# Four runs of 18 attention products between the groups of h's products, instead of two runs of 36

## The chip, the cores and the metric

The kernel runs on one core of one Trainium2 chip. The core has a matrix engine (PE, with its weight loads shown apart as PEld), a vector engine (DVE), a scalar engine (ACT), a general engine (POOL) and a synchronising engine (SP) which here issues the DMA transfers. Each engine takes its instructions in the order in which the program was written, and waits at an instruction until the semaphores that it names have been raised by other engines or by landed transfers.

The metric is the device time of one execution, in microseconds (us). Less is better. Beside the times there is one profiled execution, of which the trace keeps every instruction's start and duration.

## The reference

The program computes attention in which small scores are dropped, and feeds its result to a two-layer network. All data are float32.

```python
# attention: 8 batches, 8 heads, 576 tokens, 64 numbers per head
scores = scale * np.matmul(q, k.transpose(0, 1, 3, 2))
thresh = np.max(scores, axis=-1, keepdims=True) - tau
scores = np.where(scores >= thresh, scores, -1000000000.0)
attn   = softmax(scores)                       # over the 576 keys
x      = np.matmul(attn, v)                    # -> 4608 tokens x 512
# network on 4608 tokens: 512 -> 1024 -> 512
h    = x @ w_in
solu = h * softmax(h)
ln   = (solu - mean) / np.sqrt(var + 1e-06) * g_ln
out  = ln @ w_out
```

What this case is about are the products `attn @ v` (called pv here) and `x @ w_in` (called h).

## The kernel before

**Units.** The 576 tokens of a batch are cut into two blocks of 256 and a rest of 64. In the code a unit of attention is (batch `b`, `kind`, pair of heads `hp`): kinds 0 and 1 are the two blocks of 256 tokens, with four pairs of heads each, and kind 2 is the rest of 64 tokens for all eight heads at once. Each unit takes two slots (`slots`, line 367), so a batch has 18 slots and the program 144.

**Rounds.** The main loop (line 820) makes one round per slot. A round first writes PE's score products of its slot (`scores`, line 376), then DVE's row minimum (line 420), ACT's threshold and exponential (lines 435 and 444), POOL's division by the sum for the slot before (lines 451 to 454) and DVE's 32x32 block transposes of that (line 466). When both slots of a unit are transposed, SP issues the transfers that put the blocks in their places in `wT` (lines 475, 477, and 482 for kind 2). The four transfers of line 482 each fill one half of `wT`'s partitions: two fill the lower half, two the upper half. Products with v of the lower half (`u` = 0) wait for the first two, those of the upper half (`u` = 1) for the others.

**What PE does beside the scores.** In each round PE also takes one step of the network: a half of h (`ff_h`, `("h", 0)` and `("h", 1)`) or a half of the output (`ff_o`), in the cycle h, h, o, o. In the rounds with a step of h, when a unit's products with v are due (three rounds after its last slot, line 716), PE takes those as well (`attend_steps`, line 486, 36 instructions for kinds 0 and 1, 72 for kind 2). As a rule h's 16 products come first and all of pv's after them. For kind 2 alone, pv's instructions are handed to `ff_h` as a generator `beside` and drawn from it between h's groups.

**h's groups.** `ff_h` computes 512 of the 1024 columns of h for 128 tokens in four groups (`c` = 0 to 3) of four instructions, each on one 64x64 quarter of the PE array. All instructions around the change work on such quarters, four at a time, and every float32 instruction stands in the trace as two passes, so that 16 instructions of h are 32 records and 36 of pv are 72. The instructions of h are 512 columns long, those of kind 2's pv 64.

**PSUM.** h and pv are accumulated in two buffers of PSUM called p0 and p1 (`take`, line 104), which are handed from user to user in the order in which they are freed. A pv's buffer is freed by ACT's copy of its result (`attended`, line 537), the output's by ACT's copy at line 690, h's by DVE at line 600.

**Fence.** After the first half of h (part 0) POOL writes a small mark (`fence`, line 109) once the last four products are done. The first product of part 1 waits for this mark (line 575). After part 1 DVE takes the row maximum of h (line 585).

The last round's units are taken by an ending (from line 831) in which `ff_h` is called without a split and returns before it draws from `beside`.

Of the kernel before, what the change touches and what calls it, by code (L numbers as in the profile page):

```python
# [20 lines left out]
def kernel(  # L21
# [82 lines left out]
    def take(name):  # L104
        tag = pairs_free.pop(0)
        return tag, ps_mm.tile([P, 1024], F32, tag=tag, name=name)


    def fence(first):
        m = nc.gpsimd.memset(mark, 0.0)  # L110
        for mm in first:
            sync(m, mm)
        return m

    def sync(late, first):
        tc.add_manual_dep(
            late.ins, first.ins.name,
            mybir.DependencyInfo(mybir.DependencyClass.Sync, mybir.DependencyReason.DATA),
            reason="rows change banks",
        )  # L120
# [365 lines left out]
    def attend_steps(key):  # L486
        b, kind, hp = key
        unit = units[key]
        wT = unit["wT"]
        unit["y"] = take("pv")  # L490
        _, y = unit["y"]
        y = y.rearrange("p (u n) -> p u n", u=2)

        for e in range(2) if kind == 2 else [None]:
            for m in range(NK):
                for u in range(2):
                    d, h0 = source(b * NP + (hp if e is None else e + 2 * u))
                    for h in range(2):
                        if e is None:
                            to = y[ROWS[h], u, 0:P].rearrange("p (g r x) -> p g r x", r=2, g=2)  # L500
                            rhs = wT[ROWS[u], :, m, :, h]
                        else:
                            to = y[ROWS[h], u, 64 * e : 64 * e + 64].rearrange(
                                "p (g x) -> p g x", g=2
                            )
                            rhs = wT[ROWS[u], :, m, e, h]
                        nc.tensor.matmul(  # L507
                            out=to,
                            lhsT=d["v"][
                                ROWS[u], (h0 + h - u) % 4, m,  # L510
                            ],
                            rhs=rhs,
                            start=m == 0, stop=m == NK - 1,
                        )
                        yield
# [25 lines left out]
    def tokens(t):  # L541

        if len(t) == 1:
            return xe[t[0]]
        b, kind, m = t
        return xh[b, kind][:, :, P * m : P * m + P]


    def ff_h(t, part, split, beside=()):
        beside = iter(beside)  # L550
        x = tokens(t)
        if part == 0:
            tag, h = take("h_ps")
            ffn[t] = dict(h=h, tag=tag, split=split)
        d = ffn[t]
        h = d["h"]
        if not d["split"]:
            f = slice(512 * part, 512 * part + 512)
            for c in range(NP):
                nc.tensor.matmul(  # L560
                    out=h[:, f], lhsT=x[:, c], rhs=w1_parts[:, c, part],
                    start=c == 0, stop=c == NP - 1,
                )
            return
        last = []
        for c in range(NP):
            for r in range(2):
                f = slice(512 * (part ^ r), 512 * (part ^ r) + 512)
                for y in range(2):
                    mm = nc.tensor.matmul(  # L570
                        out=h[ROWS[y], f], lhsT=x[ROWS[r], c, ROWS[y]], rhs=w1_parts[ROWS[r], c, part ^ r],
                        start=part == 0 and c == 0, stop=part == 1 and c == NP - 1,
                    )
                    if part and not last:
                        sync(mm, d["fence"])
                    last.append(mm)
            for _, _ in zip(range(36 * (c > 1)), beside):
                pass
        if part == 0:
            d["fence"] = fence(last[-4:])  # L580
# [193 lines left out]
    with tc.manual_schedule():  # L774
# [37 lines left out]
        rnd = 0  # L812
# [7 lines left out]
        while True:  # L820
# [84 lines left out]
            beside = ()  # L905
            if attending is not None and attending[1] == 2 and step is not None:
                beside = attend_steps(attending)
            if step == ("h", 0):
                ff_h(cur, 0, rnd + 1 < NS, beside)
                quarter = 1  # L910
            elif step == ("h", 1):
                ff_h(cur, 1, None, beside)
                quarter = 2
                by = rnd + 2 * (rnd == 14)
# [102 lines left out]
```

## Time and profile before

| what | value |
|---|---|
| median of 3 runs | 855.63 us (854.59, 855.63, 858.16) |
| the profiled execution's own time | 855.96 us |
| its span, from the first to the last instruction | 854.2 us |
| PE busy | 819.7 us, 96% of the span |
| DVE, ACT, POOL busy | 680.4, 572.3, 499.1 us (80, 67, 58%) |
| pv's passes of 64 columns | 1152 passes, 21.8 us busy in all |
| h's passes (both forms of line 570) | 2048 passes |
| transfers into `wT`, issue to landing | median 6.7 us (288 KB) and 5.5 us (576 KB) |

The span is what lies between the first and the last instruction on the core; the execution's own time is 1.8 us longer. Busy time of PE counts a stretch in which at least one matmul is in flight; a matmul's record is longer than the step between two matmuls on one quarter, so a short wait need not show as idle time.

Kind 2's pv is found in the trace as the passes of 64 columns on line 507. They stand at eight places, one per batch, which begin at 120.8, 214.0, 308.4, 410.7, 505.7, 609.2, 702.2 and 798.5 us.

### The profile page before, as it was taken

To read this page: it belongs to the slowest core of one execution; us is meant where nothing else is said; L and a number is where in the kernel's file an instruction comes from. 1 tells how busy PE (TensorE), PEld (TensorE's weight loads), DVE (VectorE), ACT (ScalarE), POOL (GpSimd) and SP (SyncE) were. 2 spreads that over 40 slices of the span, in tenths; PEclk is the share of its full clock that TensorE was granted. 3 is DMA by queue.
4 is the path that set the end of the run, shared out by engine and by line. 5 is a ranking of instruction groups with operands and counts; after the bars stand their busy time and mean duration, and the time that the engine had idled before them with its cause. 6 is when DMAs were issued, how large, how long until landed. Compare 5 with 4: busy or idle time off the path is not lost.

```text
span 854.2 us, 36120 instructions
## 1 busy us (share of the span) xinstructions
PE 819.7 (96%) x15363; PEld 613.4 (72%) x15363; DVE 680.4 (80%) x1241; ACT 572.3 (67%) x1127; POOL 499.1 (58%) x945
## 2 busy tenths in 40 slices
PE   6679889999999999999999999999999999999997
PEld 5456666667677787777688877777777777777655
DVE  6999868889788888888788878888888888787361
ACT  6888857877666666666676667766667777775121
POOL 3888637666556656565566666565666655555120
PEclk8889999999999999999999999999999999999999
DMA  9989897898889788887889787888888887655212
GB/s 339 265 236 231 208 206 185 227 250 208 225 208 227 194 191 205 219 214 181 216 212 220 194 177 200 212 212 212 200 207 228 202 195 188 154 136 140 67 39 63
DMA packets 75442, 168.54 MB, mean 197 GB/s; under 512 B 11274, under 2 KB 32786, under 8 KB 75282
## 3 DMA queue, kind: packets, MB, share of 16 engines
q1 hardware_dynamic: 74994, 165.82, 77.3%
q8 instruction: 120, 1.97, 1.0%
q10 hardware_dynamic: 288, 0.43, 0.2%
q14 instruction: 40, 0.33, 0.1%
HBM read 46.14 MB, written 9.44 MB: 65 GB/s over the span
## 4 chain that ended last, share of the span: by engine, by line
PE 80%; DVE 7%; DMA 6%; ACT 3%; issue 2%; POOL 1%; SPq 1%; DVEq 0%; ACTq 0%
PE o_ps L675 27%; PE h_ps L570 21%; PE s_ps L399 15%; PE pv L507 14%; DMA wT<-T 4%; PE h_ps L560 3%; DVE T L466 2%; DVE w L420 2%; ACT w L435 1%; ACT w L444 1%; DVE w L290 1%; DMA V<-u 1%; POOL w L454 0%; PE tp L336 0%; SPq L482 0%
## 5 line engine op out<-in xcount | busy, mean ns | idle before, releaser
L435 ACT ACTIVATE w<-s_ps,nth 128x576 f32<-128x576 f32 x280 | 196.9, 738 | 110.5 <-DVE nth L420 92.0
L675 PE MATMUL o_ps<-w,uT 64*64 64x256 f32 x4608 | 268.4, 376 | 1.3 <-DVE uT L662 0.6
L675 PEld LDWEIGHTS o_ps<-w,uT 64*64 64x64 f32 x4608 | 221.0, 133 | 55.2 <-ACT xh L537 12.0
L420 DVE CUSTOM_DVE_ANT_0 w<-s_ps,tau_t 128x576 f32<-128x576 f32 x280 | 200.1, 751 | 73.7 <-PE s_ps L399 46.3
L454 POOL TENSOR_SCALAR w<-w,sm 128x576 f32<-128x576 f32 x288 | 221.3, 780 | 14.3
L466 DVE STREAM_TRANSPOSE T<-w 128x576 f32<-128x576 f32 x288 | 207.7, 756 | 24.4 <-POOL w L454 23.7
L570 PE MATMUL h_ps<-w,xh 64*64 64x512 f32 x1856 | 220.4, 590 | 0.0
L444 ACT ACTIVATE w<-w,ntau 128x576 f32<-128x576 f32 x288 | 219.5, 766 | 0.0
L507 PEld LDWEIGHTS pv<-wT,v 64*64 64x64 f32 x5760 | 170.4, 135 | 40.7 <-issue 22.9
L399 PE MATMUL s_ps<-kT,qT 64*64 64x64 f32 (+1 forms) x2048 | 173.5, 415 | 16.6 <-ACT w L435 12.5
L507 PE MATMUL pv<-wT,v 64*64 64x128 f32 (+1 forms) x5760 | 173.1, 263 | 7.2 <-DMA wT<-T 5.0
L570 PEld LDWEIGHTS h_ps<-w,xh 64*64 64x64 f32 x1856 | 114.5, 133 | 81.4 <-issue 52.1
L451 POOL TENSOR_SCALAR sm<-sm 128x2 f32<-128x2 f32 x144 | 36.2, 252 | 194.5 <-ACT w L444 191.1
L452 POOL TENSOR_TENSOR sm<-sm,mone 128x2 f32<-128x2 f32 x144 | 108.2, 751 | 12.0
L399 PEld LDWEIGHTS s_ps<-kT,qT 64*64 64x64 f32 x2048 | 70.5, 137 | 25.4 <-ACT w L435 18.0
L537 ACT COPY xh<-pv 128x256 f32<-128x256 f32 x64 | 25.4, 397 | 72.5 <-PE pv L507 72.4
L636 ACT ACTIVATE V<-u,nb,rs 128x1024 f32<-128x1024 f32 x36 | 44.7, 1241 | 41.3 <-POOL nb L626 34.8
L662 DVE STREAM_TRANSPOSE uT<-V 128x1024 f32<-128x1024 f32 x36 | 44.3, 1231 | 21.4 <-DMA V<-u 20.7
L444 ACT ACTIVATION_READ_ACCUMULATOR w<-w,ntau 128x1 f32 x288 | 55.3, 192 | 0.0
L600 DVE TENSOR_TENSOR u<-h_ps,u 128x1024 f32<-128x1024 f32 x36 | 42.8, 1189 | 9.9 <-ACT u L594 9.9
L641 DVE TENSOR_SCALAR u<-u,rs,nb 128x1024 f32<-128x1024 f32 x36 | 34.9, 969 | 17.5 <-ACT V L636 17.4
L594 ACT ACTIVATE u<-h_ps,hm 128x1024 f32<-128x1024 f32 x36 | 40.2, 1117 | 9.9 <-DMA V<-u 5.6
(81 smaller groups left out, 563.7 us busy)
## 6 DMA issues: line engine op xcount, KB each, us to landing
wT<-T SPq DMA_DIRECT2D x160, 288.0 KB, 6.7
wT<-T SPq DMA_DIRECT2D x64, 576.0 KB, 5.5
v<-in_v_dram SPq DMA_DIRECT2D x16, 576.0 KB, 5.7
V<-u SPq DMA_DIRECT2D x144, 64.0 KB, 3.4
out_dram<-ob SPq DMA_DIRECT2D x71, 128.0 KB, 2.6
q<-in_q_dram SPq DMA_DIRECT2D x28, 288.0 KB, 6.0
k<-in_k_dram SPq DMA_DIRECT2D x27, 288.0 KB, 6.5
qT<-flip SPq DMA_DIRECT2D x48, 144.0 KB, 3.5
```

The lines of the kernel that those rows point to most:

```text
L399: nc.tensor.matmul(out=ps[h][ROWS[y], ks], lhsT=lhsT, rhs=d["kT"][ROWS[h], ks], start=True, stop=True,)
L420: nc.vector.tensor_tensor_reduce(out=w, in0=ps[:, 0:S], in1=(zero if loose else tau_t).to_broadcast([P, S]), scale=1.0, scalar=BIG, op0=AL ...
L435: nc.scalar.activation(out=d["w"][x], in_=d["w"][x] if d["loose"] else d["ps"][x][:, 0:S], func=AF.Prelu, bias=d["nth"][x], scale=-1.0, al ...
L444: nc.scalar.activation(out=w, in_=w, func=AF.Exp, bias=ntau, scale=1.0, accum_out=sm[:, x : x + 1])
L452: nc.gpsimd.tensor_tensor(out=sm, in0=sm, in1=mone, op=ALU.pow)
L454: nc.gpsimd.tensor_scalar(out=w, in0=w, scalar1=sm[:, x : x + 1], scalar2=1.0, op0=ALU.mult, op1=ALU.mult)
L466: nc.vector.transpose(out=T[:, :, r, h, :], in_=w)
L507: nc.tensor.matmul(out=to, lhsT=d["v"][ROWS[u], (h0 + h - u) % 4, m,], rhs=rhs, start=m == 0, stop=m == NK - 1,)
L570: mm = nc.tensor.matmul(out=h[ROWS[y], f], lhsT=x[ROWS[r], c, ROWS[y]], rhs=w1_parts[ROWS[r], c, part ^ r], start=part == 0 and c == 0, st ...
L636: nc.scalar.activation(out=V, in_=u, func=AF.Identity, bias=nb, scale=rs)
L662: nc.vector.transpose(out=uT, in_=d["V"].rearrange("p y (m x) -> p m y x", x=32))
L675: nc.tensor.matmul(out=d["o"][ROWS[z], 512 * (r ^ other) : 512 * (r ^ other) + 256], lhsT=d["uT"][ROWS[r], m].rearrange("p y x -> p (y x)" ...
```

## The change

`ff_h` drew 36 of `beside`'s instructions after each of its last two groups (`c` = 2 and 3) and none after the first two. From round 31 on it draws 18 after each of its four groups.

```diff
@@ ff_h
                     if part and not last:
                         sync(mm, d["fence"])
                     last.append(mm)
-            for _, _ in zip(range(36 * (c > 1)), beside):
+            for _, _ in zip(range(18 if rnd > 30 else 36 * (c > 1)), beside):
                 pass
         if part == 0:
             d["fence"] = fence(last[-4:])
```

In the built program this changes the order of PE's instructions at six places, those of batches 1 to 6. There PE had 12 instructions of h, 36 of pv, 4 of h, 36 of pv; it now has four times 4 of h and 18 of pv. Batch 0's place lies before round 31, and batch 7's lies in the ending, where its 72 instructions of pv stand in one run before and after. Of the six places, the 1st, 3rd and 5th hold part 0 of h, and the 2nd, 4th and 6th part 1. The order of the instructions on DVE, ACT, POOL and SP is the same as before, and no instruction is added or removed. The mark at part 0 and the row maximum at part 1 still wait for h's last product, which now stands 18 instructions of pv ahead of the end of the step instead of 36.

## The prediction

> **What bounds the kernel now.** I read the page's shares of busy time first, then the waits and busy time of PE between 130 and 850 us, then the timeline at the six places that the change touches.
>
> ```profile
> PE 819.7 (96%) x15363; PEld 613.4 (72%) x15363; DVE 680.4 (80%) x1241; ACT 572.3 (67%) x1127; POOL 499.1 (58%) x945
> 130.00:850.00 720.00, 715.18 (x13348) 1.00 0.77 189
> PE s_ps L399 <- issue: 2.4, 2, 1.3
> PE pv L507 <- DMA wT<-T: 1.1, 2, 0.8
> PE pv L507 <- ACT w L444: 0.3, 1, 0.3
> ```
>
> In the second line a stretch of 720 us holds 715.18 us of busy PE at full clock (1.00); the last three lines are all that PE waited for in it. So PE is the bound, and time that is put on PE there comes out at the end, unless one of these few waits shrinks for it.
>
> Next, how the touched runs lie on PE. From each run's first pass to the next run's first pass, 24 passes of h (12 instructions) take 2.575 us, 8 take 0.860, and the 72 passes of 36 products with v take 1.048. These are the shortest values over the places, most of which have them exactly. A run begins where the one before ends by its own step: switching costs nothing that the records show, and so a finer interleaving has nothing to win there.
>
> Then the waits at the start of pv. Of place 4 and place 1:
>
> ```profile
> 503.10 3.01 PE L570 MATMUL h_ps<-w,xh 64*64 64x512 f32 x24
> 505.67 0.74 PE L507 MATMUL pv<-wT,v 64*64 64x64 f32 x9
> L507 PEldq EVENT_SEMAPHORE  x2: 51/1043/2035, 503.1 to 505.2; - x2
> 506.09 0.21 PEld L507 LDWEIGHTS pv<-wT,v 64*64 64x64 f32 x8 [0.28 <-DMA wT<-T]
> ...
> 211.03 2.85 PE L570 MATMUL h_ps<-w,xh 64*64 64x512 f32 x24
> 213.56 0.36 ACT L537 COPY xh<-pv 128x256 f32<-128x256 f32 x1
> 213.98 0.33 PEld L507 LDWEIGHTS pv<-wT,v 64*64 64x64 f32 x13 [0.99 <-ACT xh L537]
> ```
>
> At place 4 PE's sequencer came to pv's wait at 503.12, when all 24 passes of h were queued and only the first had begun, and stood there for 2035 ns until the lower half of wT had landed. PE did not notice: it had 2.6 us of h to run. The upper half came later still and held the third product until 506.09. At place 1 the wait was for PSUM: ACT's copy, which frees the buffer, ended at 213.92. The eight products of h that the change moves behind pv are what covers these waits.
>
> **The change, part by part.** Nothing is added or removed; at six places, pv's start is moved ahead of 8 of the 12 instructions of h that stood before it. They take 2.575 - 0.860 = 1.715 us. So pv falls due 1.715 us sooner at each place. If what it waits for comes no sooner, PE stands for that time, the 8 instructions follow afterwards, and the step ends 1.715 us later. What it waits for does not depend on the order of h and pv: wT comes from scores of rounds before, and the copy that frees the buffer from a pv before. The times below are starts of h in the timeline, plus 0.86 for the new due time, and the landings of the four transfers in the semaphore updates of the trace.
>
> Place 1: h at 211.03, due 211.89, buffer free 213.92: the start stays at 213.98. Loss 1.715.
> Place 2: h at 305.79, due 306.64, lower half 307.58, upper half 308.82. The third product stood at 308.96 and stays there. Loss 1.715.
> Place 3: h at 408.11, due 408.97, halves at 407.09 and 408.53, buffer at 408.30: ready 0.4 us ahead. No loss.
> Place 4: h at 503.10, due 503.96, halves at 505.12 and 506.05: the third product stays at 506.09. Loss 1.715.
> Place 5: h at 606.66, due 607.52, halves at 605.72 and 606.91, buffer at 606.85: ready 0.6 us ahead. No loss.
> Place 6: h at 699.58, due 700.44, halves at 700.77 and 702.00. The third product stood at 702.20, unhindered; after a landing at 702.00 it starts at about 702.12 (place 2 took 0.14 from landing to start, place 4 0.04). Loss 1.64.
>
> Direct sum: 3 x 1.715 + 1.64 = 6.78 us. Next, what comes back. After place 1 the profile shows:
>
> ```profile
> 217.97 3.70 PE L570 MATMUL h_ps<-w,xh 64*64 64x512 f32 x32
> 221.97 0.44 PE L507 MATMUL pv<-wT,v 64*64 64x128 f32 x4 [0.30 <-ACT w L444]
> 222.65 2.07 PE L507 MATMUL pv<-wT,v 64*64 64x128 f32 x66 [0.24 <-DMA wT<-T]
> ```
>
> This h took 4.00 us to the start of pv where the others take 3.433, and this pv 2.485 to the next scores where the others take 1.965: 1.09 us of waiting for a wT that SP issued from 214.53 on, without regard to place 1. A PE that is late by 1.715 no longer meets this wait, and 0.63 is left of place 1. Behind places 2, 4 and 6 there is no wait that PE could skip: between 311 and 415, 509 and 608, and 704 and 850 us PE's only wait is one of 1.2 us put down to "issue". So 6.78 - 1.09 = 5.7.
>
> Then the cut at 18. It is no multiple of four, so that after the first run two quarters of the array have two passes more than the others (2 x 58 ns = 0.12 us), which the next run evens out. The trace has no such run. Bounds: nothing, if the quarters keep the skew, to 0.12 twice at each of six places = 1.4 us. The nearest row is place 2, where the lower quarters got one pair of passes (0.12) ahead through the wait, and began the following h 0.07 ahead (309.95 against 310.03): 0.05 of a skew was lost. I take 0.05 a place, 0.3 us. The Trainium skill (TensorEngine Tiling (Array Packing), Key Properties) says that tiles of the array run independently; by it the cut costs nothing and the sum would be 5.7. The row of place 2 speaks for most of that, not all.
>
> Other queues. Their order is the same, but POOL's mark (odd places) and DVE's row maximum (even places) wait for h's last product, which, counted from the step's end, comes 18 products or 0.52 us later. Behind the mark POOL has the division of line 451, and it had been idle for 0.57 us ahead of the mark at place 3; PE needs the mark for its next half of h, which loaded weights at 416.11 (414.85 without the wait of 1.26 ahead of it), when a mark 0.52 later would have been done at 413.54. At place 4 DVE did the maximum at 508.26 and next had work at 511.70; at places 2 and 6 it began after a transpose which ended later than h. I cost these at nothing; without that cover each is 0.52 us a place, 3.1 us in all.
>
> Sum: 5.7 + 0.3 = 6.0 us. On the profiled execution's own 855.96 (span 854.2 and 1.8 around it) this is 862.0; that execution lies 0.33 above the median of 855.63, so the forecast is 861.8, between the two ways of adding.
>
> **The rivals.**
>
> *Instruction supply gives it back* (ends on the other side: not slower). PE's two longest waits after 130 us, 1.26 us at 416.1 and 1.15 at 510.5, wait for nothing that the profile shows. Should they be instructions that arrive late, a sequencer that stands 2 us at pv's wait at 503 to 506 gives supply the time to get ahead. Both gone are 2.4 us: 859.4. It decides from 1.7 us on, where the loss falls under 0.5% (4.28 us of 855.63, about what a measurement of this kernel can tell from no change). Against it: the one at 416.1 follows a place where I expect no stand. Chance 0.13.
>
> *Earlier landings.* At places 1, 3 and 5 the upper half landed 1.15, 0.43 and 0.25 us after h's start; at 2, 4 and 6 it was 3.03, 2.95 and 2.42. If these three depend on chance traffic and land as at place 1, they cost about 0.4 each: 0.63 + 1.2 + 0.3 gives 858.1. Against it: odd and even places alternate without exception. Chance 0.06.
>
> *The clock falls.* PE's granted clock halved in some stretches of 3.41 us near the start:
>
> ```profile
> 23.28:26.69 3.41, 1.30 (x13) 1.00 1.03 261
> 26.70:30.10 3.40, 3.12 (x32) 0.50 1.05 208
> 57.41:60.82 3.41, 1.54 (x32) 1.00 0.90 243
> ```
>
> A stretch with 2.11 us idle was followed by one at 0.50; one with 1.87 us idle was not. Place 1 would leave PE idle from h's last end, 212.16, to 213.98, 1.82 us; places 2, 4 and 6 less (1.6, 1.4, 1.1, in two pieces). One fall costs half of 3.41 us: 863.5. Chance 0.10. The Trainium skill (TensorE: Matmul & The Clock Gate, Part 1: The HAM clock gate) has the clock fall after a whole idle window of about 3.4 us; by that rule none of these stands could do it, and this rival would be out. The rows above differ from the page: 2.11 us were enough.
>
> *More of the waits bind.* Place 1's 1.09 us doesn't come back, and the waits at places 3 and 5 land 1 us later: 855.8 + 6.0 + 1.1 + 1.1 = 864.0. Chance 0.05.
>
> *Shorter runs are faster.* pv's four passes step at 58.2 ns where 64 of h's columns take 53.6; if weight loads cause the difference and h's neighbourhood hides them, 4.6 ns x 36 steps x 6 places = 1.0 us is won, and with no wait binding it ends at 854.8, inside 0.5%. To be faster by over 0.5%, 3.3 us more would have to come from elsewhere. Chance 0.02. That the change doesn't do what it says is excluded by the built program's order.
>
> **How the numbers follow.** The forecast has 0.62: 861.8, and 860.0 to 863.3 by itself (landings move by some tenths of a microsecond at three places). The range reaches down to the earlier landings, 858.1, and up to 864.2, past the clock's case and the last but one; about 1 in 10 is left outside. Slower by over 0.5% needs 859.9: 0.60 of the forecast's 0.62, the clock, the further waits and 0.02 of the others: 0.77. Within 0.5%: 0.21, the rest of those. Faster: 0.02, for what no row speaks of.
>
> **What would show it.** In the trace of the changed kernel: the third product with v at places 2, 4 and 6 about 3 us after the start of h, as before, with two fewer groups of h ahead of it; idle PE ahead of it put down to the transfers into wT, and at place 1 to ACT's copy; at places 3 and 5 no idle time; the wait at 222 gone; PE's busy time for lines 507 and 570 the same. The prediction is wrong if wT comes with pv's new due time, if PE stands for it but the end is not later, or if the halves' waits at places 3 and 5 bind too.

## The result, and the profile after

The changed kernel takes 862.57 us (median of 19 runs, 857.47 to 873.72), the kernel before in the same sitting 856.49 us (19 runs, 854.59 to 860.33). The ratio is 1.0056, with a 95% interval of 1.0037 to 1.0076: slower by about 4.8 us (3.2 to 6.5). The ratio leaves out the changed kernel's two longest runs (871.17 and 873.72 us), which belong to a slower state; the medians of all runs lie 6.1 us apart.

The runs spread more than the effect. Part of that spread arises before any changed code is reached: the start of h at place 1 lies at 211.03 us in the profile of before, and between 209.34 and 217.63 us over all the profiles of this study. So I compare profiles from the start of h at place 1 to the end of the span. Before: 854.17 - 211.03 = 643.14 us. After: 855.68 - 210.18 = 645.50 us, 2.36 more. (The profiled execution of after took 857.47 us, the fastest of its 19.)

This line of the page of after has the engines' busy time and instructions:

```profile
PE 821.7 (96%) x15363; PEld 617.4 (72%) x15363; DVE 680.8 (80%) x1241; ACT 571.9 (67%) x1127; POOL 500.1 (58%) x945
```

The same instructions, and PE again the bound. This is one window of its trace (stretch, its length, PE busy and its instructions, granted clock, DMA share, GB/s):

```profile
130.00:850.00 720.00, 713.57 (x13320) 1.00 0.76 189
```

And these are all of PE's waits between 130 and 850 us (line waited at, releaser: us in total, times, longest):

```profile
PE pv L507 <- DMA wT<-T: 4.2, 6, 1.0
PE pv L507 <- ACT xh L537: 1.8, 1, 1.8
PE s_ps L399 <- ACT w L435: 0.2, 1, 0.2
```

PE was idle for 6.43 us of the 720, against 4.82 before. The waits have changed places: 2.4 us put down to "issue" are gone, the waits for the transfers into `wT` grew from 1.1 to 4.2 us, and one of 1.8 us for ACT's copy is new.

The timeline at places 1 and 4 shows the lost cover (start, us, passes, idle time before and its releaser):

```profile
210.18 1.13 PE L570 MATMUL h_ps<-w,xh 64*64 64x512 f32 x8
...
213.13 0.81 PE L507 MATMUL pv<-wT,v 64*64 64x64 f32 x36 [1.82 <-ACT xh L537]
213.73 1.07 PE L570 MATMUL h_ps<-w,xh 64*64 64x512 f32 x8
...
503.43 1.29 PE L570 MATMUL h_ps<-w,xh 64*64 64x512 f32 x8
504.79 0.33 PE L507 MATMUL pv<-wT,v 64*64 64x64 f32 x4
505.87 0.69 PE L507 MATMUL pv<-wT,v 64*64 64x64 f32 x32 [0.74 <-DMA wT<-T]
506.38 1.04 PE L570 MATMUL h_ps<-w,xh 64*64 64x512 f32 x8
```

Where 24 passes of h stood, 8 do now; then PE has nothing to do for 1.82 us at place 1. At place 4 it does the four passes of the lower half and stands until the upper half has landed, 2.40 us after h's start. It had stood for the lower half too: pv was due 0.86 us after h's start and began after 1.36, which does not show as idle time because the records of h run to 504.72. The other 16 passes of h, which had filled that time, come afterwards. At place 5 nothing is late, and the four runs go through:

```profile
606.74 1.13 PE L570 MATMUL h_ps<-w,xh 64*64 64x512 f32 x8
607.59 0.75 PE L507 MATMUL pv<-wT,v 64*64 64x64 f32 x36
608.16 1.04 PE L570 MATMUL h_ps<-w,xh 64*64 64x512 f32 x8
609.02 0.69 PE L507 MATMUL pv<-wT,v 64*64 64x64 f32 x34
```

The table has the length of the step at each place, from the start of h to the next scores, in us:

| place | before | after | difference | predicted |
|---|---|---|---|---|
| 1 | 5.97 | 7.68 | 1.71 | 1.715 |
| 2 | 6.08 | 7.27 | 1.19 | 1.715 |
| 3 | 5.53 | 6.50 | 0.97 | 0 |
| 4 | 5.90 | 7.06 | 1.16 | 1.715 |
| 5 | 5.53 | 5.53 | 0 | 0 |
| 6 | 5.53 | 6.95 | 1.42 | 1.64 |
| sum | 34.5 | 41.0 | 6.46 | 6.78 |

Of these 6.46 us, 1.40 come back between places 1 and 2: from one h to the next it takes 94.76 us before and 95.07 after, only 0.31 more although place 1 is 1.71 longer. The wait at 222 is gone. And both "issue" waits of before, 1.26 us at 416.1 and 1.15 at 510.5, are gone: 2.41. That makes 6.46 - 1.40 - 2.41 = 2.65, where the two profiles differ by 2.36. Counted from one h to the next, the changed kernel takes 0.31, 1.19, -0.32, -0.25 and 0.00 us more than before, and from place 6 to the end 1.43: the losses of places 3 and 4 (0.97 and 1.16) are gone again by the next place, on the way to which before had its two "issue" waits. The experiments had to say whether all of this is lost cover, whether the cut itself costs anything, and whether the two "issue" waits really went because of the change, which was one of the rivals.

### The profile page after: what moved, and what is told of

Read it like the earlier page. It is cut to its first block, busy times and chain, and to the rows that moved or that the text cites. A ratio compares the mean times of both kernels' runs of the same rounds, so it can differ in the third digit from the quotient of the medians.

```text
span 855.7 us, 36120 instructions
## 1 busy us (share of the span) xinstructions
PE 821.7 (96%) x15363; PEld 617.4 (72%) x15363; DVE 680.8 (80%) x1241; ACT 571.9 (67%) x1127; POOL 500.1 (58%) x945
## 4 chain that ended last, share of the span: by engine, by line
PE 80%; DMA 8%; DVE 4%; ACT 3%; POOL 2%; SPq 2%; issue 1%; DVEq 0%; ACTq 0%
PE o_ps L675 26%; PE h_ps L570 22%; PE s_ps L399 14%; PE pv L507 14%; DMA wT<-T 6%; PE h_ps L560 3%; SPq L482 1%; DVE w L420 1%; ACT w L444 1%; ACT w L435 1%; DVE T L466 1%; DMA raw<-in_moe_w_in_dram 1%; POOL w L454 0%; DMA V<-u 0%; POOL sm L451 0%
## 5 line engine op out<-in xcount | busy, mean ns | idle before, releaser
L675 PEld LDWEIGHTS o_ps<-w,uT 64*64 64x64 f32 x4608 | 229.9, 133 | 47.6 <-ACT xh L537 12.3
L507 PEld LDWEIGHTS pv<-wT,v 64*64 64x64 f32 x5760 | 172.3, 136 | 51.6 <-issue 33.7
L507 PE MATMUL pv<-wT,v 64*64 64x128 f32 (+1 forms) x5760 | 176.1, 263 | 9.5 <-DMA wT<-T 7.2
L399 PE MATMUL s_ps<-kT,qT 64*64 64x512 f32 (+1 forms) x2048 | 171.9, 415 | 11.7 <-ACT w L435 11.0
L570 PEld LDWEIGHTS h_ps<-w,xh 64*64 64x64 f32 x1856 | 109.0, 133 | 79.6 <-issue 57.0
L585 DVE TENSOR_REDUCE hm<-h_ps 128x1 f32<-128x1024 f32 x36 | 42.9, 1192 | 8.9 <-PE h_ps L570 6.1
```

The costliest lines, as they stand in the source:

```text
L399: nc.tensor.matmul(out=ps[h][ROWS[y], ks], lhsT=lhsT, rhs=d["kT"][ROWS[h], ks], start=True, stop=True,)
L507: nc.tensor.matmul(out=to, lhsT=d["v"][ROWS[u], (h0 + h - u) % 4, m,], rhs=rhs, start=m == 0, stop=m == NK - 1,)
L570: mm = nc.tensor.matmul(out=h[ROWS[y], f], lhsT=x[ROWS[r], c, ROWS[y]], rhs=w1_parts[ROWS[r], c, part ^ r], start=part == 0 and c == 0, st ...
L675: nc.tensor.matmul(out=d["o"][ROWS[z], 512 * (r ^ other) : 512 * (r ^ other) + 256], lhsT=d["uT"][ROWS[r], m].rearrange("p y x -> p (y x)" ...
```

## The experiments

Each diff is against the changed kernel, in `ff_h`, unless it shows another place. "From place 1 on" means from the start of h at place 1 to the end of the span of that run's profile (643.14 us before, 645.50 after). Ratios are to the kernel before on the same chip, with their 95% interval.

### One part of h each

```diff
-            for _, _ in zip(range(18 if rnd > 30 else 36 * (c > 1)), beside):
+            for _, _ in zip(range(18 if rnd > 30 and part == 0 else 36 * (c > 1)), beside):
```

> The four runs of 18 only at places 1, 3 and 5 (part 0 of h); places 2, 4 and 6 as before. Theory (pv loses the cover of 8 products of h, and PE stands where what pv waits for lands later than pv's new due time): place 1 ends its step 1.7 us later and gets 1.1 to 1.4 us of it back at the next pv's wait, place 5 costs nothing, place 3 between 0 and 1.0 us by the landing of wT: 0.3 to 1.6 us in all, within 0.5%. Rival (the cuts themselves cost, more runs and more changes between h and pv): each place costs the same, a half of the 6.1 us between the medians, 3.0 us, and the step at place 5 is longer than 5.53 us.

The second kernel has `part == 1` in the same place.

> The four runs of 18 only at places 2, 4 and 6 (part 1 of h); places 1, 3 and 5 as before. Theory: the third product with v stands until the upper half of wT has landed, 2.4 to 3.0 us after the start of h, with 0.86 us of h ahead of it: each step 1.2 to 1.7 us longer, 3.6 to 5.1 us in all, about 0.5% slower, nothing got back behind them. Rival (the cuts themselves cost): 3.0 us, as many as at the odd places.

| places in four runs | ratio | from place 1 on | steps at places 1 to 6 |
|---|---|---|---|
| 1, 3, 5 | 1.003 (1.000 to 1.006) | 643.60 | 7.67, 6.99, 5.53, 5.62, 5.53, 5.53 |
| 2, 4, 6 | 1.0041 (1.0008 to 1.0075) | 645.62 | 5.96, 7.63, 5.53, 7.40, 5.53, 7.29 |

Each place pays for itself: place 1 is longer by 1.70 us in the one, and places 2, 4 and 6 by 1.55, 1.50 and 1.76 in the other, while places 3 and 5 are at 5.53 in both kernels, and places left as they were keep before's step or less (place 1 5.96 for 5.97, place 4 5.62 for 5.90, place 6 5.53). The ratio of the first kernel alone would not decide: 1.003 is 2.6 us, with an interval from 0 to 5.2, which holds both the 0.46 us of its profile and the 3.0 us of the rival. What speaks against the rival are the steps of 5.53 us at places 3 and 5. One step does not fit: place 2 in the first kernel has before's order and took 0.91 longer, because its upper half landed 3.95 us after h's start (3.04 before). Landings move by such amounts without any edit at that place.

PE's waits for "issue" from 205 us on, first in the kernel with places 1, 3 and 5, then in that with 2, 4 and 6:

```profile
PE s_ps L399 <- issue: 1.9, 2, 1.0
```

```profile
PE s_ps L399 <- issue: 1.0, 1, 1.0
```

Before had 2.41 us. With "issue" left out, the first lost 641.70 - 640.73 = 0.97 us and the second 644.61 - 640.73 = 3.88. Their sum, 4.85, is what after lost by the same count: 645.50 - 640.73 = 4.77.

### The same order with nothing to wait for

Here pv of the last 64 tokens multiplies v by a constant from round 31 on, not by the attention weights; the transfers still run, but PE no longer waits for them.

```diff
+    fixed = const.tile([P, 2, 32], F32, name="fixed")
+        nc.gpsimd.memset(fixed, 1.0 / 576)
...
-                            rhs = wT[ROWS[u], :, m, e, h]
+                            rhs = fixed[ROWS[u]] if rnd > 30 else wT[ROWS[u], :, m, e, h]
```

> The changed kernel's order, but from round 31 on the products with v of a batch's last 64 tokens read a constant in place of wT (left out: these tokens' weights, so their outputs are not the reference's; the transfers into wT are still made). Nothing is left to wait for at places 2 to 6 but PSUM. Theory (the transfers into wT are what PE stands for): steps at places 2 to 6 of 5.53 us where the changed kernel had 6.5 to 7.3, place 1 still 7.7; from the start of h at place 1 to the end within 0.7 us of before, and the waits put down to issue, 2.4 us before the change and none after it, are back at places 3 and 4, because the sequencer does not stand there any more. Rival (order and cuts cost, the transfers are only named by the profile): steps stay at 6.5 to 7.3 us. Second rival on the issue waits (they are chance and have nothing to do with PE's standing): they may be absent here too.

The second kernel has the same edit with the order of before (`36 * (c > 1)`).

> The same constant in place of wT with the order of before (two runs of 36; these tokens' weights are left out here too). Theory: steps of 5.53 us at places 2 to 6, as in the run before this one, so that the two orders take the same time to within 0.5 us once nothing is waited for, place 1 apart (1.7 us more there in the order of 18, most of which comes back at the next pv). Against the kernel before it is 0.9 us shorter at places 2 and 4. Rival (order and cuts cost): it is faster than the order of 18 by 3 us or more.

| order | ratio | from place 1 on | steps at places 1 to 6 |
|---|---|---|---|
| four runs of 18 | 0.9969 (0.9938 to 0.9999) | 642.74 | 9.35, 6.14, 5.53, 5.53, 5.53, 5.65 |
| two runs of 36 | 0.9984 (0.9962 to 1.0005) | 643.12 | 5.97, 5.76, 5.59, 5.53, 5.53, 5.53 |

Place 4 of the first, in the timeline:

```profile
504.11 1.09 PE L572 MATMUL h_ps<-w,xh 64*64 64x512 f32 x8
504.96 0.74 PE L509 MATMUL pv<-fixed,v 64*64 64x64 f32 x35
```

A full run follows 0.85 us after h's start, and the step is 5.53 us, where after needed 7.06. With the transfers out of the way, four runs of 18 are no slower than two of 36. The totals alone would not show it, since "issue" waits are 1.32 us in the one and 3.85 in the other; the steps at places 3 to 5 do. So what costs time is the wait, not the interleaving; and the cut at 18 costs nothing that can be seen (places 3, 4 and 5 are at 5.53, the shortest step of before). Place 2's 0.61 above that holds a wait of 0.39 us for "issue" inside its third run, and the rest, 0.22, is there with two runs of 36 too (5.76). Place 1 keeps its wait for ACT's copy, which the constant doesn't touch, and its step of 9.35 is longer than after's 7.68: that is the next experiment.

All waits of the four-run kernel from 205 us on:

```profile
PE pv L509 <- ACT xh L539: 1.8, 1, 1.8
PE h_ps L572 <- issue: 0.9, 1, 0.9
PE pv L509 <- issue: 0.4, 1, 0.4
```

With the stands gone an "issue" wait is back at place 3 (0.93 us at 417.69), but none at place 4, where it was expected too.

### Place 1 and the clock

The changed kernel once more, as it is:

> The changed kernel once more, for a second look at two things of which one profile tells too little. Theory: steps at places 2, 4 and 6 of 6.9 to 7.4 us again, place 5 at 5.53, place 3 between 5.5 and 6.5 by the landing; PE's waits put down to issue are absent or short wherever PE has stood for wT by 0.7 us or more at place 3 or 4, and are there (0.8 to 1.3 us) where it has not. Rival: the issue waits come and go by chance and turn up here with the stands, in which case the changed kernel is 4 to 5 us slower from place 1 to the end and not 2.4.

It gave a ratio of 1.0046 (1.0017 to 1.0075) and 647.86 us from place 1 on, 2.36 more than the first profile of after. Its steps are 9.35, 7.35, 6.43, 7.52, 5.53 and 7.17: place 1 alone is 1.67 us longer. From place 1 to place 2 it took 96.74 us, 1.98 more than before.

Windows around the stand at place 1, of the first profile of after:

```profile
210.08:213.49 3.41, 1.59 (x32) 1.00 0.65 171
213.49:216.90 3.41, 3.41 (x123) 1.00 0.68 141
```

and of the second:

```profile
210.50:213.91 3.41, 1.57 (x44) 1.00 0.41 104
213.91:217.32 3.41, 3.41 (x67) 0.50 0.90 211
```

In the second the clock halved for 3.41 us right behind the stand: 67 passes in a stretch in which the first had 123. Half of 3.41 is 1.7. The kernel with the constant and four runs fell at the same place, that with places 1, 3 and 5 did not:

```profile
211.04:214.45 3.41, 1.57 (x48) 1.00 0.76 194
214.45:217.86 3.41, 3.41 (x58) 0.50 0.82 190
```

```profile
210.84:214.25 3.41, 1.60 (x49) 1.00 0.50 124
214.25:217.66 3.41, 3.41 (x111) 1.00 0.91 206
```

1.57 us of busy PE in the stretch ahead went with a fall twice, 1.59 and 1.60 without one. That is no bound: the row of before at 57.41, shown in the prediction, had 1.54 and no fall, and the kernel at the end of this part has a fall behind a stretch with 1.88. What else decides isn't in the trace. The Trainium skill (TensorE: Matmul & The Clock Gate, Part 1: The HAM clock gate) lets the clock fall only after an idle window of about 3.4 us; here 1.84 us of idle time in such a stretch (3.41 - 1.57) were enough, in two profiles, and the measurement decides.

Then all places but the first, with place 1 as before:

```diff
-            for _, _ in zip(range(18 if rnd > 30 else 36 * (c > 1)), beside):
+            for _, _ in zip(range(18 if rnd > 45 else 36 * (c > 1)), beside):
```

> The four runs of 18 at places 2 to 6 only; place 1 as before. In two of the four profiles so far in which PE stood at place 1 (1.84 us idle) its clock was halved for the 3.41 us behind it, which made place 1's step 9.35 us in place of 7.68. Theory (the fall of the clock comes from place 1's stand, and no other stand is long enough in one piece): no fall of the clock between 130 and 850 us, place 1 at 5.97 us, steps at places 2, 4 and 6 of 6.9 to 7.6, from place 1 to the end 2 to 3.5 us more than before's 643.1 (less by the lost issue waits). Rival (any place can bring the clock down): a fall of the clock behind place 2 or 4.

The ratio is 1.0034 (1.0005 to 1.0064), from place 1 on 646.78 us: 3.64 more than before, a little above what was expected. The steps are 5.99, 7.52, 5.53, 7.64, 5.53 and 7.02, and no fall of the clock lies behind place 1 or a later place. But the expected absence after 130 us did not come true: there is one ahead of place 1, where the program is that of before.

```profile
164.35:167.76 3.41, 1.88 (x36) 1.00 1.01 250
167.76:171.17 3.41, 3.41 (x70) 0.50 0.95 224
```

In the stretch ahead of it PE waited 1.15 us for a `wT` of another unit. The second profile with one run of 72, below, has such a fall too, at 169.98, behind a stretch with 1.54 us of busy PE. So the clock also falls at stands that the change doesn't touch. Each of these two profiles has a further fall between 115 and 135 us, which is part of why place 1 starts at 216.38 and 217.63 us in them and at 209.34 to 213.37 in the others. Of the four profiles with four runs of 18 at place 1 (the two of after, that with the odd places, that with the constant), two have a fall right behind it; none of the nine others has one there. That makes place 1's stand the likely cause of those two falls, as far as so few profiles can show it, and this kernel shows that a loss remains without place 1.

### The waits put down to "issue"

Does a PE that stood at its step skip the "issue" waits that follow? Three more orders vary how long it stands. All 72 instructions of pv in one run after the last group:

```diff
-            for _, _ in zip(range(18 if rnd > 30 else 36 * (c > 1)), beside):
+            for _, _ in zip(range(72 * (c == 3) if rnd > 30 else 36 * (c > 1)), beside):
```

> From round 31 on all 16 products of h first and then all 72 of pv: the cover is 0.86 us longer than before the change. Theory: the waits that were left before the change go (0.55 us at place 2, 0.36 at place 4; 0.38 at place 1, which comes back at the next wait): 0.9 us faster than before, ratio about 0.999. It ends slower if h's last product, which then comes sooner, or the lack of h behind pv matters. Rival (cuts cost): with one run in place of two the gain is larger, 1.5 us or more, and the steps at places 3 and 5 are shorter than 5.53 us.

The kernel with three runs of 24 has `24 * (c > 0) if rnd > 30 else 36 * (c > 1)` instead.

> From round 31 on 8 products of h ahead of the first pv in place of 4 (or 12 before the change), then 24 of pv after each of the last three groups: cover of 1.72 us, half of what the change took away given back. Theory: place 1's step 0.86 us longer than before, coming back at the next wait; places 2, 4 and 6 each 0.6 to 0.86 us longer than before, places 3 and 5 at 5.53: without the waits put down to issue 1.8 to 2.6 us more than before from place 1 to the end, where the changed kernel had 4.8. Rival (number of runs costs): three runs in place of two or four, 2.4 us spread over all six places, odd ones too.

The kernel before was run again as it is, and the one run of 72 too:

> The kernel before once more. Theory: places 3 and 5 at 5.53 us, place 1 at 5.97, places 2, 4 and 6 between 5.53 and 6.5 by the landing of wT; a wait put down to issue of 0.8 to 1.3 us after each of places 3 and 4, since PE stands at neither; no fall of the clock between 130 and 850 us. Rival on the issue waits (chance): one or both absent. Its time should be that of before: ratio 1.000.

> All 16 products of h first from round 31 on, once more, because its ratio was 0.998 with an interval that includes 1. Theory: 0.9 us faster by the waits at places 2 and 4, less what longer runs of short products add to the issue waits (3.2 us in its first profile, 2.4 before): between 0.997 and 1.001. If it is 0.998 again, with 1 outside the interval of the two together, it beats both kernels.

| order | ratio | from place 1 on | "issue" waits in it | steps at places 1 to 6 |
|---|---|---|---|---|
| 72 | 0.9981 (0.995 to 1.0012) | 643.01 | 3.16 | 5.97, 5.76, 5.53, 5.62, 5.53, 5.53 |
| 72, again | 1.0005 (0.9982 to 1.0027) | 642.74 | 2.34 | 5.98, 5.78, 5.53, 5.61, 5.53, 5.53 |
| 3 x 24 | 1.0003 (0.9972 to 1.0034) | 643.64 | 1.14 | 6.84, 6.49, 5.53, 6.86, 5.53, 6.44 |
| 36 + 36, before again | 1.0001 (0.9975 to 1.0026) | 642.82 | 2.96 | 5.98, 5.59, 5.53, 5.60, 5.53, 5.69 |

From before to three runs, 8 passes of cover go (0.86 us): places 1, 4 and 6 are longer by 0.87, 0.96 and 0.91 and place 2 by 0.41. With "issue" left out that kernel lost 642.50 - 640.73 = 1.77, and the measured difference from place 1 on is only 0.50, because its "issue" waits are 1.27 us shorter than before's. One run of 72 wins 0.88 by that count and nothing in the whole; its ratio was 0.998 and then 1.0005, so that no order tried with all its products beats the kernel before by more than the measurement can tell. Place 1 kept its step of 5.97, although its wait was expected to go: with all of h first, h's own last group waits there for the same copy by ACT, since it reads what that copy writes (weight loads of PE in the first kernel with 72):

```profile
216.34 0.21 PEld L570 LDWEIGHTS h_ps<-w,xh 64*64 64x64 f32 x8 [1.00 <-ACT xh L537]
```

All of PE's waits for "issue" from 205 us on, in the first kernel with one run of 72, and in the second profile of before:

```profile
PE s_ps L399 <- issue: 2.1, 2, 1.3
PE o_ps L675 <- issue: 1.0, 1, 1.0
```

```profile
PE s_ps L399 <- issue: 2.6, 2, 1.9
```

Over all thirteen profiles: after place 3 there is an "issue" wait of 0.78 to 1.87 us in the ten in which PE did not stand there, and none in the two of the changed kernel, in which it stood some 0.9 us. (The remaining one, the finer cut below, had no stand there but a step 1.4 us longer, and has no such wait after either place.) After place 4 there is none in the four in which the step was longer by 1.5 us or more than 5.53; 0.36 where it was longer by 1.33; and 0.70 to 1.29 in six where it was longer by up to 0.4. (Before again has 1.87 and 0.70, outside the 0.8 to 1.3 that were expected for both.) Against this stands the kernel with the constant and four runs, which had no stand at place 4 and no such wait. So a stand mostly takes the place of a wait that would have come anyway. That PE's instructions arrive late after so many short ones would fit, but what PE's sequencer waits for isn't recorded, and this cause is only argued. It can't be the whole of it: behind places 5 and 6, with the same 72 short instructions, no profile has such a wait, with a stand or without.

### A finer cut

Here pv goes in four runs of 18 too, but two of them between the single products of h's last group, so that 12 products of h stay ahead of pv as before.

```diff
                     last.append(mm)
+                    if rnd > 30 and c == 3 and len(last) in (13, 15):
+                        for _, _ in zip(range(18), beside):
+                            pass
-            for _, _ in zip(range(18 if rnd > 30 else 36 * (c > 1)), beside):
+            for _, _ in zip(range(18 * (c > 1) if rnd > 30 else 36 * (c > 1)), beside):
```

> From round 31 on 12 products of h as before, then 18 of pv, 1 of h, 18, 2 of h, 18, 1 of h, 18: pv starts where it did before the change, but in four runs of 18 with as many changes between h and pv as in the changed kernel. Theory (only the lost cover costs): within 0.3 us of the time before, steps at places 3 and 5 at 5.53 us. Rival (cuts cost): as slow as the changed kernel, +6 us, steps at places 3 and 5 of 6 us or more.

The ratio is 1.0049 (1.0015 to 1.0084), from place 1 on 650.30 us, 7.16 more than before. That was meant to show that short runs cost nothing when the cover stays, and it failed. The windows of place 3, in before and in this kernel (stretch, its length, busy time and instructions of PE, PEld, DVE, ACT and POOL, granted clock, DMA share, GB/s):

```profile
408.11:413.64 5.53, 5.53 (x179) 4.05 (x174) 3.87 (x8) 4.20 (x8) 4.35 (x11) 1.00 0.92 221
```

```profile
412.81:419.77 6.96, 6.96 (x177) 4.53 (x173) 3.88 (x8) 4.21 (x8) 3.92 (x9) 1.00 0.85 209
```

PE is busy throughout, at full clock, with the same work, and takes 1.43 us longer; place 5 shows the same 6.96. The timeline of place 3 says how:

```profile
415.97 0.59 PE L570 MATMUL h_ps<-w,xh 64*64 64x512 f32 x1
415.98 0.38 PE L507 MATMUL pv<-wT,v 64*64 64x64 f32 x7
416.40 0.59 PE L570 MATMUL h_ps<-w,xh 64*64 64x512 f32 x1
416.83 0.58 PE L507 MATMUL pv<-wT,v 64*64 64x64 f32 x25
```

The products of h that stand alone between runs of pv occupy only some of the four quarters, and the others, after a few short passes, take up no more until these are done. The edit changed two things at once, the length of the runs and the balance of the quarters, so it isn't evidence against the lost cover. That runs of 18 cost nothing by themselves is shown by the constant instead.

## Why the prediction was right, and where it was not

The forecast was 861.8, the median is 862.57, and the time lies inside the forecast's own range. But the sum is not the one I wrote down, and that it came out so close is in part luck: the lost cover was right in kind and size, the terms of place 3 and of the cut were wrong, and the waits that went and the clock that fell, neither of them in the sum, pull against each other.

*Lost cover: right, and shown.* Place 1 lost 1.71 for 1.715, in after and again (1.70) where only the odd places were changed. Places 2, 4 and 6 lost 1.19, 1.16 and 1.42, less than predicted, since counted from h's start the upper halves landed 0.2 to 0.55 us sooner than before (2.51, 2.40 and 2.20 us, against 3.04, 2.95 and 2.42). That is the scatter of landings, not the change: in the second profile of before they are at 2.51 at place 2 and 2.65 at place 6. The constant in place of `wT` removes these losses without a change of order.

*Place 3: wrong.* "No loss" was 0.97 us in after, and 6.43 - 5.53 = 0.90 in its second profile, since the upper half landed 1.75 and 1.67 us after h's start and not 0.43. It was assumed that the landing at this place would stay as one profile of before had it, with a margin of 0.4 us. The second profile of before has 0.61, which would still have been early enough. In the kernel with places 1, 3 and 5, and in that with all but place 1, there was no loss there (5.53): the half landed 1.65 and 0.06 us ahead of h's start. SP had issued its transfer 6.98 and 6.72 us ahead of h in these two, and only 5.86 and 5.64 in the two profiles of the full change. The two of before have nearly the same issue as those (5.94 and 5.92), but 6.36 and 6.53 us from issue to landing where the full change has 7.61 and 7.31. Why both of its profiles have this stays open. Place 5 was right.

*What comes back: right, a little too small.* 1.40 in place of 1.09 us, and 1.40 again in the second profile of the changed kernel and in the kernel with places 1, 3 and 5.

*The cut at 18: wrong by its whole size.* "0.05 a place" is 0: place 5 takes 5.53 us in after, and places 3, 4 and 5 with the constant. Here the rule that the prediction set against its row (the Trainium skill, TensorEngine Tiling (Array Packing), Key Properties) gave the better term: nothing.

*The mark and the row maximum: costed at nothing, and nothing shows.* Both act behind the step, so the way from one h to the next shows it: from place 5, which has the mark, it is 92.92 us before and after, and behind places 2 and 6, which have the maximum, it grew by 1.19 and 1.43 us, as the steps did (1.19 and 1.42).

*Instruction supply, a rival at 0.13: came true in part.* Its mark was that both "issue" waits go, 2.4 us. They are gone in both profiles of the changed kernel. The objection, that the first follows a place without a stand, fell with place 3. It did not bring the time back to no change, because the rest of the loss stayed.

*The clock, a rival at 0.10: came true in one of two profiles of the changed kernel,* for 1.67 us where 1.7 was put down.

So the two rivals, which I had set apart, work together and against each other. In the profiles from place 1 on, the changed kernel lost 2.36 us without the fall and 647.86 - 643.14 = 4.72 with it, against a ratio that means 3.2 to 6.5. The forecast of 6.0 had neither term, and the timing's centre of 4.8 lies nearer to it than either profile does. How often the clock falls at place 1 in the other executions isn't known. Their mean granted clock is on record: in the sitting of the second profile it is 0.9840 over ten executions of the changed kernel and 0.9842 over 31 of the kernel before, which is no sign of more falls; but one fall takes only 0.002 off an execution's mean (1.7 of 858 us), and single executions lie between 0.977 and 0.990. So the clock is not shown to make up the difference, and what the timing has above the profiles, if anything, isn't accounted for.

## What to carry to other kernels

Work that stands ahead of a waiting product covers that wait even where the profile shows no idle time: look at when the engine's sequencer reaches the wait and when the data land, not only at the idle times, before spreading such work out. Interleaving wins nothing on an engine that switches between kinds of work at no cost and has no wait to fill. A new stand can also swallow a later wait, so the losses of several places should not be added without asking which later waits go with them; and one execution's landings say little about a margin of a few tenths of a microsecond.

## What the runs showed of the hardware that was not expected

- PE's clock halved for 3.41 us behind a stretch of 3.41 us with 1.57 us of busy PE, at place 1 in two profiles, and ahead of place 1 behind stretches with 1.88 and 1.54 us. Behind stretches with 1.54, 1.59 and 1.60 us it did not. A stretch in which PE was idle for 1.5 to 1.9 us of 3.41 went with a fall in some profiles and with none in others.
- The quarters of PE don't run freely apart: with single products of h of 512 columns in some quarters between short runs in all of them, a step took 6.96 us in place of 5.53 with PE never idle. A skew of two short passes (64 columns) between quarters, as after a run of 18, cost nothing. The Trainium skill (TensorEngine Tiling (Array Packing), Key Properties) has tiles operate independently; the short skew agrees with that, and the long one shows that it has a limit.
- After the steps with pv's 72 short instructions at places 3 and 4, PE mostly has a wait of 0.7 to 1.9 us that the profile puts down to nothing but "issue", unless it stood before; after those at places 5 and 6, with as many, no profile has one.
